# One piece of V per batch loaded into the lower 64 partitions of two slots, in transfers of 8 rows

## The chip, the cores and the metric

The kernel runs on one core of one Trainium2 chip. The metric is device time in microseconds for one execution. Before the change three runs took 1097.45, 1098.14 and 1099.65 us; the median is 1098.14.

## The reference

Eight sequences (B = 8) with one token each (width D = 448) pass through attention, a small MLP block, the same attention and the same MLP again. The attention has 16 query heads on 8 KV heads of 256 dimensions, over a cache of 4096 positions:

```python
q = (x @ wq).reshape(B, 1, 16, 256).transpose(0, 2, 1, 3)
k = jnp.repeat(k_cache, 2, axis=1)              # k_cache: (8, 8, 4096, 256) bf16
v = jnp.repeat(v_cache, 2, axis=1)
p = softmax(einsum("bhqd,bhkd->bhqk", q, k) / 16)
o = einsum("bhqk,bhkd->bhqd", p, v)             # then @ wo, added to x

x = x + attention(layernorm(x)); x = x + mlp(layernorm(x))
x = x + attention(layernorm(x)); x = x + mlp(layernorm(x))
```

Both attentions use the same caches, of 134 MB each. In the MLP of one token the shifted parts of the first half are zero, so that what is left of it is a normalisation, a 448 x 1792 product, a gelu, a 1792 x 448 product and the residual.

## The kernel before, in words

**Pieces and slots.** K or V of one KV head of one batch is 4096 positions x 256. Partition p holds positions 32p to 32p + 31, so that one partition's share is 16 KB in a row of memory. It is cut into four pieces (`c` = 0 to 3) of 128 partitions x 4096 bytes, 512 KB each (`chunks`, L444). Pieces land in 31 slots of SBUF (`NSLOT`, L13), each 128 partitions x 4096 bytes. One, two or four pieces that follow each other can come in one DMA (512 KB, 1 MB, 2 MB) if slots side by side are free. All loads are issued by SyncE (SP), on one queue.

**Order of the work.** Heads are taken in pairs: m = 0 to 3 stands for KV heads 2m and 2m + 1, with s = 0, 1 for the two. For batch b the kernel computes scores, softmax and the product with V in layer 0 (`kpart`, `vpart` with `layer` = 0), then `turn(b)` (output sum, MLP, next query), then layer 1. What was transposed of K for m = 1 to 3 stays in its slots for layer 1; K for m = 0 and all of V are loaded again. Loads of K and V are woven with each other (`weave`, L1213). Layer 1's V for m = 0 of batch b is woven with the first K of batch b + 1 (L1241); for the last batch it comes at the end (L1245).

**A planner decides order and slots.** Every operation is an entry with a cost, a due time and what it depends on (`Plan.add`), every load a `Unit` (L73) with a slot. `Plan.schedule` (L168) runs through the entries in simulated time and writes down the order of each engine's instructions, the slot of each load and the waits. A load is issued when its slots are free, that is when the last reader of what they held has run; it occupies SP for 330 ns in the plan (L292). A group of loads that finds no run of free slots can be split (L266 to L275). So a small change of one cost or one load can move instructions and slots elsewhere.

**K.** Most pieces of K are rearranged by VectorE in blocks of 32 x 32 (L914) and then multiplied on TensorE (L923); some are transposed by TensorE (L832), copied back by ScalarE (L892) and multiplied (L902).

**Softmax.** The scores of a pair lie in PSUM as 128 columns. The exponentials go to `pT` (L1006). In the order that pieces rearranged by VectorE need, they are transposed once more by TensorE and VectorE (L1013, L1021); for pieces that keep their natural order they are computed again into `pT` (L1027), or copied to `pN`, a small tile of which there are two (L399, L1010).

**V.** The product with V in this part of the kernel (L1077 to L1092) takes a 128 x 8 block of exponentials as weights and 512 columns of V as the moving operand, four matmuls per piece, and accumulates in a bank of `psV` over both heads:

```python
w = pN[z][:, 12 * i + 4 * s:12 * i + 4 * s + 8] if own_(s, c) else pT[y][:, o:o + 8]
v = slots[u.slot].rearrange("p (k j d) -> p j k d", k=2, j=4)[:, i]
last = e.matmul(psV[x][32 * i:32 * i + 8, :].rearrange("p (k d) -> p k d", k=2), w, v,
                start=(s == 0 and c == 0), stop=(s == 1 and c == NCH - 1))
```

Another form (L1063) takes V as weights.

**Semaphores.** Each slot has one, which a load raises by 16 when it has landed; a reader waits for the slot's running total (L1264).

Of the kernel before, what the change touches and what calls it, by code (L numbers as in the profile page):

```python
# [3 lines left out]
P = 128  # L4
B = 8
# [6 lines left out]
NCH = 4  # L12
NSLOT = 31  # L13
SMALL = 218
SLOT = 2048
# [5 lines left out]
NN = ((1, 0, 1, 1), (0, 0, 1, 1))  # L21
NZ = 2
WIDE = ((1, 0),)
MOST = (4, 4, 4, 2)
DRY4 = 4000.0
STILL = (False, False)
# [46 lines left out]
class Unit:  # L73


    def __init__(self, name, emit, nbytes, slotted=True):
        self.name, self.emit, self.nbytes, self.slotted = name, emit, nbytes, slotted
        self.wide = None
        self.slot = self.sem = self.val = None
        self.op = None  # L80
        self.readers = []
        self.land = None
        self.evs = [None, None]
        self.raw, self.source = False, None
        self.group, self.lead, self.pair = [self], None, None


class Plan:
# [79 lines left out]
    def schedule(self, order, nslot):  # L168
# [8 lines left out]
        free = {e: 0.0 for e in ("pe", "dve", "act", "pool", "sp")}  # L177
# [68 lines left out]
        while remaining or nxt[0] < len(order):  # L246
# [8 lines left out]
            while nxt[0] < len(order):  # L255
                u = order[nxt[0]]
                if any(d.end is None for d in u.op.deps):
                    break
                start = max(free["sp"], max((d.end + 80 for d in u.op.deps), default=0.0))
                us = u.group  # L260
                if u.slotted:
                    if len(us) == 1:
                        best = single(t)
                    else:
                        best, short = run(t, len(us))
                        if short and len(us) == 4 and transfer < t + DRY4:  # L266
                            order.insert(nxt[0] + 1, self.split(u, users))
                            us = u.group
                            best, short = run(t, len(us))
                        one = single(t)  # L270
                        if (len(us) == 2 and short and transfer < t + DRY and one is not None and slot_free[one][0] <= t + 1e-6
                                and len(slot_free) > bool(raw or u.raw) + sum(1 for o in ready["act"] if o.target is not None)
                                and free["sp"] <= t + 1e-6):
                            order.insert(nxt[0] + 1, self.split(u, users))
                            us, best = u.group, one  # L275
                    held = sum(1 for x in {o.target for o in ready["act"] if o.target is not None} if x.slot is None)
                    if best is None or len(slot_free) < len(us) + bool(raw or u.raw) + held:
                        break
                    start = max([start] + [slot_free[best + k][0] for k in range(len(us))])
                if start > t + 1e-6:  # L280
                    sp_next = start
                    break
                if u.slotted:
                    for k, x in enumerate(us):
                        _, waits = slot_free.pop(best + k)
                        x.slot = best + k
                        for w in waits:
                            u.op.deps[w] = True
                        live.append(x)
                        if x.raw:  # L290
                            raw.add(x)
                free["sp"] = start + 330.0  # L292
                if u.emit is not None:
                    transfer = max(start + 3300.0, transfer) + (P * 4096 * len(us) / 415.0 if len(us) > 1 else u.nbytes / 410.0)
                    land = transfer + 2000.0
                else:
                    land = start
                for x in us:
                    x.land = land
                u.op.on = "sp"  # L300
                seq["sp"].append(u.op)
                done(u.op, land, 0.0)
                nxt[0] += 1
                progress = True
            for e in ("pe", "dve", "act", "pool"):
# [15 lines left out]
                o = min(cand, key=lambda o: (o.prio, o.name))  # L321
# [37 lines left out]
def bass_interleave_layers__gqa_block_cached__mixer_s_mlp__decode_kernel(  # L359
# [26 lines left out]
    slots = [slab[:, SLOT * i:SLOT * i + SLOT] for i in range(NSLOT)]  # L386
# [6 lines left out]
    ident = sb("ident", [P, P], bf)  # L393
# [3 lines left out]
    pT = [sb(f"pT{i}", [P, 192], bf) for i in range(NP)]  # L397

    pN = [sb(f"pN{i}", [P, 48], bf) for i in range(NZ)]  # L399
# [17 lines left out]
    psS = [nc.alloc_psum_tensor(f"psS{i}", [P, 512], f32) for i in range(NS)]  # L417
    psV = [nc.alloc_psum_tensor(f"psV{i}", [P, 512], f32) for i in range(NV)]
# [7 lines left out]
    plan = Plan()  # L426
# [14 lines left out]
    U_wo = [rows(f"wo{i}", wo_sb[:, 8 * i:8 * i + 8, :], wo_src[:, 8 * i:8 * i + 8, :], P * 7168 * 1.1) for i in range(4)]  # L441
    U_w4 = [rows("w4", w4_sb[:, :, :], B_w4.rearrange("(t m) n -> m t n", m=P), P * 12544 * 1.1)]

    def chunks(cache, b, h, name, skip=(), most=2):  # L444


        src = cache[b, h].rearrange("(p j) d -> p (j d)", p=P)

        def emit(e, u):
            c, n = int(u.name[-1]), len(u.group)  # L450
            return e.dma_start(slab[:, SLOT * u.slot:SLOT * (u.slot + n)], src[:, SLOT * c:SLOT * (c + n)])
        us = [None if c in skip else Unit(f"{name}{c}", emit, P * 4096) for c in range(NCH)]
        for i in range(0, NCH, most):
            group = [u for u in us[i:i + most] if u is not None]
            if len(group) == most:
                plan.load(group[0], mates=group[1:])
            else:
                for u in group:
                    plan.load(u)
        return us  # L460


    Bc = Buf()
# [350 lines left out]
    def apart(t):  # L814

        return t.rearrange("p (a c u r) -> p a c r u", a=4, u=3, r=4)[:, :, :, :, 0:3:2]
# [19 lines left out]
    def kpart(at, layer, b, m, kept, most=2):  # L836
# [12 lines left out]
        nS[0] += 1  # L849
        p.x = x  # L850
        p.y = y = free_p.pop(0)
        p.z = z = free_n.pop(0) if layer == 0 and m > 1 else None
        plan.prio = at
        p.K, p.kload = [], []
        for s in range(2):
# [169 lines left out]
        for c in range(nn if z is None else 0):  # L1025
            ss = slice(sum(c >= w for w in nns), 2)
            add("act", lambda e, c=c, ss=ss: e.activation(apart(pT[y])[:, :, c, :, ss], xs.rearrange("p (a c r s) -> p a c r s", a=4, c=4, r=4)[:, :, c, :, ss],  # L1027
                                                          ACT.Exp, scale=INV_SQRT_DH), 230, [], [BpT[y]], [bS[x]], prio=pr, name=n + f"pn{c}")
        add("pool", lambda g: g.partition_all_reduce(db, rs, P, ReduceOp.add), 450, [B_["pm"]], [B_["gm"]], prio=pr + 1, name=n + "db")
        R = add("dve", lambda e: e.reciprocal(rc, db), 70, [B_["gm"]], [Brc[y]], prio=pr + 1, name=n + "rc")  # L1030
        R.deps = {d: data or d.eng == "dve" for d, data in R.deps.items()}
# [2 lines left out]
    def vpart(at, p, still, bank, most, aside):  # L1034
# [2 lines left out]
        own_ = lambda s, c: z is not None and c < p.nns[s]  # L1037
        Bp = lambda s, c: [BpN[z]] if own_(s, c) else [BpT[y], BpZ[y]]
        plan.prio = at
        p.V = [u for s in range(2) for u in chunks(A_v_cache, b, 2 * m + s, f"{n}V{s}", (), most)]  # L1040
        p.vload = [u for u in p.V if u.lead is None]
        if layer == 0:
            out_, bo = o1[b % 2][:, 8 * m:8 * m + 8], Bo1[b % 2][m]
        else:
# [28 lines left out]
        else:  # L1073
# [3 lines left out]
            for s in range(2):  # L1077
                for c in range(NCH):
                    u = p.V[NCH * s + c]

                    def pv(e, u=u, c=c, s=s):
                        for i in range(4):
                            o = 12 * (NCH * i + p.place(s, c)) + 4 * s
                            w = pN[z][:, 12 * i + 4 * s:12 * i + 4 * s + 8] if own_(s, c) else pT[y][:, o:o + 8]
                            if c < p.nns[s]:
                                v = slots[u.slot][:, 512 * i:512 * i + 512].rearrange("p (k d) -> p k d", k=2)
                            else:
                                v = slots[u.slot].rearrange("p (k j d) -> p j k d", k=2, j=4)[:, i]
                            last = e.matmul(psV[x][32 * i:32 * i + 8, :].rearrange("p (k d) -> p k d", k=2), w, v,  # L1089
                                            start=(s == 0 and c == 0), stop=(s == 1 and c == NCH - 1))  # L1090
                        return last
                    o = add("pe", pv, 430, Bp(s, c), [], [bV[x]], [u], prio=at + 0.02 * (NCH * s + c), name=f"{n}V{s}{c}", n=4)  # L1092
                    if s or c:
                        o.deps[first] = True
                    else:
                        first = o
# [24 lines left out]
                for d in Bq1[b].readers + Bq1[b].writers:  # L1121
                    O.deps.setdefault(d, False)
        free_p.append(y)
        if z is not None:
            free_n.append(z)

    Bst = [{k: Buf() for k in ("pm", "gm", "mx")} for _ in range(NS)]
    red, Bred = sf[:, 0:8], [Bs[k] for k in ("sq", "f", "f1")]
# [129 lines left out]
    for o in seq["sp"]:  # L1258
        u = o.unit
        if u.emit is None:  # L1260
            u.sem = None
            continue
        if u.slotted:
            slot_n[u.slot] += 16  # L1264
            u.sem, u.val = slot_sem[u.slot], slot_n[u.slot]
        else:
            u.sem, u.val = nc.alloc_semaphore(f"s_{u.name}"), 16
# [124 lines left out]
```

## Time and profile before

| | |
|---|---|
| profiled execution | 1098.74 us |
| its span, first to last instruction | 1095.7 us |
| TensorE, its weight loads, VectorE, ScalarE, GpSimd busy | 756.3, 526.6, 832.6, 207.8, 71.4 us |
| moved by DMA | 448.94 MB, 410 GB/s on average |
| mean granted TensorE clock | 0.619 |
| loads from V: 2 MB, 1 MB, 512 KB | 50, 149, 14 |
| loads from K: 2 MB, 1 MB, 512 KB | 44, 71, 2 |
| median time from issue to landing, V: 2 MB, 1 MB, 512 KB | 19.1, 9.7, 8.1 us |

How to read it. The page gives each engine's busy time and share of the span, then the span in 40 slices with a digit for the busy tenths. "DMA" is the mean busy share of the core's 16 DMA engines. A queue's line has its packets, its megabytes, and the time of its packets as a share of what 16 engines have in the span. A line of SyncE's own waits has the instruction that waits, who ended the wait, then the total in us, how many times, and the longest. The chain of waits follows the work that ended last back to the start, and shares the span out over what it passed through. Beside these views the trace has a record for each DMA packet (start, duration, size, queue; not which of the 16 engines) and a time for each rise of a load's semaphore; a load of 128 rows makes sixteen rises, one when each DMA engine has finished its share, and has landed with the last.

### The profile page before, as it was taken

The numbers are of one execution on the slowest core, as the hardware profiler recorded it, in microseconds if no ns is written. First come the engines' busy times: TensorE is split into PE (matmuls) and PEld (weight loads), VectorE is DVE, ScalarE is ACT, GpSimd is POOL, SyncE is SP. The second block draws the span as 40 slices with busy tenths as digits, with TensorE's granted clock in tenths as the row PEclk, the third lists the DMA queues.
The fourth block names the chain that finished last, engine by engine and source line by source line (L and its number), as shares of the span: only waits on it lengthen the run. The fifth ranks groups of instructions, "written<-read, shape, count | busy, mean of one in ns | idle before, by whom it ended". The sixth has DMA issues, their size and how long they took to land.

```text
span 1095.7 us, 33703 instructions
## 1 busy us (share of the span) xinstructions
PE 756.3 (69%) x15400; PEld 526.6 (48%) x15400; DVE 832.6 (76%) x1595; ACT 207.8 (19%) x314; POOL 71.4 (7%) x232
## 2 busy tenths in 40 slices
PE   2566586778577865867767787577666786676864
PEld 2355454465346543555436554355444654356533
DVE  4999459964997499955899469984799739995572
ACT  1032121112021211203112032121221121121210
POOL 0000000000000000000000000000100000000000
PEclk9997566556655665556655556555655566555665
DMA  9999999999999999999999999999999999999994
GB/s 353 406 419 420 395 406 426 422 412 408 429 423 415 412 425 427 421 405 409 424 426 420 411 412 429 426 417 394 427 427 423 419 399 428 427 422 411 410 427 176
DMA packets 54846, 448.94 MB, mean 410 GB/s; under 512 B 5536, under 2 KB 11568, under 8 KB 14128
## 3 DMA queue, kind: packets, MB, share of 16 engines
q1 hardware_dynamic: 54704, 446.80, 98.4%
q8 instruction: 120, 1.97, 0.7%
q14 instruction: 22, 0.18, 0.0%
HBM read 446.77 MB, written 0.01 MB: 408 GB/s over the span
## 4 chain that ended last, share of the span: by engine, by line
DVE 39%; DMA 24%; PE 21%; issue 9%; ACT 3%; POOL 0%; POOLq 0%; DVEq 0%
DVE slots L914 29%; DMA slots<-in_A_k_cache_dram 16%; DMA slots<-in_A_v_cache_dram 8%; PE psV L1089 6%; PE psS L923 5%; DVE pT L1021 2%; PE psT L678 2%; ACT slots L892 2%; PE psS L902 2%; DVE slots L1102 1%; PE psV L1063 1%; PE psT L607 1%; PE psK L832 1%; PE psT L1138 1%; DVE qe L643 1%
## 5 line engine op out<-in xcount | busy, mean ns | idle before, releaser
L914 DVE STREAM_TRANSPOSE slots<-slots 128x1024 bf16<-128x1024 bf16 x544 | 649.4, 1228 | 33.0 <-DMA slots<-in_A_k_cache_dram 24.3
L923 PE MATMUL psS<-qe,slots 128*128 128x8 bf16 x5760 | 225.3, 175 | 152.6 <-DVE slots L914 111.5
L923 PEld LDWEIGHTS psS<-qe,slots 128*128 128x128 bf16 x5760 | 191.1, 104 | 238.5 <-DVE slots L914 176.0
L1089 PE MATMUL psV<-slots,pT 128*8 128x512 bf16 x1528 | 181.1, 550 | 17.5 <-DMA slots<-in_A_v_cache_dram 9.5
L892 ACT COPY slots<-psK 128x1024 bf16<-128x1024 bf16 x80 | 78.8, 1014 | 168.0 <-PE psK L832 167.6
L832 PE MATMUL psK<-ident,slots 128*128 128x128 bf16 x640 | 74.2, 301 | 4.2 <-DMA slots<-in_A_k_cache_dram 4.1
L1100 ACT ACTIVATE slots<-psV 128x512 bf16<-128x512 f32 x48 | 29.0, 605 | 218.5 <-PE psV L1089 218.4
L985 POOL PARTITION_ALL_REDUCE small<-small x64 | 23.8, 372 | 693.5 <-DVE small L983 582.4
L832 PEld LDWEIGHTS psK<-ident,slots 128*128 128x128 bf16 x640 | 61.1, 138 | 7.0 <-DMA slots<-in_A_k_cache_dram 4.9
L1063 PE MATMUL psV<-pT,slots 128*128 128x2 bf16 x1568 | 50.9, 166 | 17.1 <-DMA slots<-in_A_v_cache_dram 15.9
L951 PE MATMUL psS<-slots,qe 128*8 128x512 bf16 x184 | 55.4, 587 | 6.7 <-DVE slots L914 5.4
L1063 PEld LDWEIGHTS psV<-pT,slots 128*128 128x128 bf16 x1568 | 47.3, 104 | 19.7 <-DMA slots<-in_A_v_cache_dram 16.1
L1089 PEld LDWEIGHTS psV<-slots,pT 128*8 128x8 bf16 x1528 | 31.5, 90 | 50.5 <-issue 20.9
L1021 DVE STREAM_TRANSPOSE pT<-psS 128x128 bf16<-128x128 bf16 x64 | 44.9, 702 | 6.5 <-PE psS L1013 4.7
L1006 ACT ACTIVATE pT<-psS 128x128 bf16<-128x128 f32 x56 | 15.5, 277 | 178.7 <-DVE psS L1003 178.6
L1066 DVE TENSOR_REDUCE small<-psV 128x8 f32<-128x32 f32 x16 | 2.8, 174 | 58.5 <-PE psV L1063 58.5
L1111 PE MATMUL psV<-same,slots 128*128 128x4 bf16 x320 | 14.0, 166 | 43.0 <-DVE slots L1102 36.9
L630 DVE TENSOR_TENSOR qe<-psT,small 128x32 bf16<-128x32 f32 x32 | 6.1, 190 | 48.2 <-PE psS L923 34.3
L902 PE MATMUL psS<-qo,slots 128*128 128x2 bf16 x768 | 27.8, 167 | 17.6 <-ACT slots L892 10.5
L1102 DVE TENSOR_TENSOR slots<-psV,slots 128x512 bf16<-128x512 f32 x48 | 32.3, 672 | 10.0 <-ACT slots L1100 10.0
L902 PEld LDWEIGHTS psS<-qo,slots 128*128 128x128 bf16 x768 | 24.0, 101 | 25.4 <-ACT slots L892 17.1
L1111 PEld LDWEIGHTS psV<-same,slots 128*128 128x128 bf16 x320 | 11.8, 102 | 49.2 <-issue 40.8
(170 smaller groups left out, 805.8 us busy)
## 6 DMA issues: line engine op xcount, KB each, us to landing
slots<-in_A_v_cache_dram SPq DMA_DIRECT2D x149, 1024.0 KB, 9.7
slots<-in_A_v_cache_dram SPq DMA_DIRECT2D x50, 2048.0 KB, 19.1
slots<-in_A_k_cache_dram SPq DMA_DIRECT2D x44, 2048.0 KB, 18.1
slots<-in_A_k_cache_dram SPq DMA_DIRECT2D x71, 1024.0 KB, 13.7
slots<-in_A_v_cache_dram SPq DMA_DIRECT2D x14, 512.0 KB, 8.1
wo_sb<-in_A_wo_dram SPq DMA_DIRECT2D x4, 896.0 KB, 19.5
wq_sb<-in_A_wq_dram SPq DMA_DIRECT2D x3, 1024.0 KB, 9.1
w_sb<-in_B_w_dram SPq DMA_DIRECT2D x1, 1568.0 KB, 16.9
```

The costliest lines, as they stand in the source:

```text
L832: last = e.transpose(tile[:, j * P:(j + 1) * P], slots[u.slot][:, o:o + P], ident[:, :])
L892: return e.copy(slots[u.slot][:, 1024 * t:1024 * t + 1024], tile)
L902: last = e.matmul(o, slots[u.slot][:, i:i + P], q, start=(cc == 0), stop=(cc == 1))
L914: return e.transpose(o, i)
L923: last = e.matmul(o, slots[u.slot][:, i:i + P], qe[:, 128 * k + 64 * s + 8 * g:128 * k + 64 * s + 8 * g + 8], start=(g == 0), stop=(g == 7))
L951: last = e.matmul(o, q, K[:, lo:hi + 1:hi - lo, :, g, :], start=(g == 0), stop=(g == 7))
L1021: add("dve", lambda e: e.transpose(pZ[:, :, 0:3:2].rearrange("p n s r -> p n r s"), psS[x][:, 128:192].bitcast(bf).rearrange("p (n r s) -> ...
L1063: last = e.matmul(o, slots[u.slot][:, i:i + P], w, start=(j == 0), stop=(j == 7))
L1089: last = e.matmul(psV[x][32 * i:32 * i + 8, :].rearrange("p (k d) -> p k d", k=2), w, v, start=(s == 0 and c == 0), stop=(s == 1 and c == ...
L1100: add("act", lambda e: e.activation(part(0), psV[x][:, :], ACT.Copy), 590, [], [Bhalf[0]], [bV[x]], [v], prio=at - 1, name=n + "ve0").targ ...
L1102: add("dve", lambda e: e.tensor_tensor(part(1), psV[x][:, :], part(0), ALU.subtract), 590, [Bhalf[0]], [Bhalf[1]], [bV[x]], [v], prio=at - ...
L1111: last = e.matmul(to[:, 4 * cc:4 * cc + 4].rearrange("p (s h) -> p s h", s=2), part(k // 2)[:, i:i + P], w, start=(k == 0), stop=(k == 3))
```

## The change

For one piece per batch (piece 3 of V of KV head 0 in layer 1, batches 0 to 6; with bf16 data 512 KB) the 128 rows no longer go to the 128 partitions of one slot. Rows 0 to 63 go to partitions 0 to 63 of one slot and rows 64 to 127 to partitions 0 to 63 of a second slot; partitions 64 to 127 of both stay unused. Each half comes in eight DMAs of 8 rows, to partitions r0, r0 + 4, ..., r0 + 28, with r0 = 0 to 3 and 32 to 35, so that 16 small DMAs take the place of the piece's share of a larger one. The other pieces of that head come at most two in one DMA.

Since V's rows 64 to 127 now lie in partitions 0 to 63, their exponentials must too: one more matmul with a part of the identity moves them down into PSUM, ScalarE copies them to a tile `pN`, and the product of this piece is eight matmuls of 64 rows instead of four of 128. The planner counts eight issues of 330 ns for each half.

```diff
+LOWS, LOWC = 0, 3
+def LOW(layer, b, m, s):
+    return s == LOWS and m == 0 and layer == 1 and b < B - 1
...
-                free["sp"] = start + 330.0
+                free["sp"] = start + 330.0 * u.issues
...
+        if low:
+            def half(p0):
+                def emit(e, u):
+                    for i in range(8):
+                        r0 = 32 * (i // 4) + i % 4
+                        d = e.dma_start(slots[u.slot][r0:r0 + 29:4, :], src[p0 + r0:p0 + r0 + 29:4, SLOT * LOWC:SLOT * (LOWC + 1)])
+                        if i < 7:
+                            d.then_inc(u.sem, 16)
+                    return d
+                return emit
+            most = 2
+            us[LOWC] = Unit(f"{name}{LOWC}", half(0), 64 * 4096)
+            us[LOWC].upper = Unit(f"{name}u{LOWC}", half(64), 64 * 4096)
+            us[LOWC].issues = us[LOWC].upper.issues = 8
...
+        p.zl = zl = free_n.pop(0) if p.low else None
...
+            low = psS[x][0:64, 192:208].rearrange("p (a r) -> p a r", a=4)
+            add("pe", lambda e: e.matmul(low, ident[:, 64:P], apart(pT[y])[:, :, p.place(LOWS, LOWC), :, LOWS], start=True, stop=True),
+                110, [BpT[y], Bc], [], [bS[x]], prio=pr, name=n + "lo", n=1)
+            add("act", lambda e: e.copy(apart(pN[zl])[0:64, :, 0, :, LOWS], low), 230, [], [BpN[zl]], [bS[x]], prio=pr, name=n + "lc")
...
+                    def low(e, u=u, c=c, s=s):
+                        for i in range(4):
+                            o, i_ = 12 * (NCH * i + p.place(s, c)) + 4 * s, 12 * i + 4 * s
+                            for w, v in ((pT[y][0:64, o:o + 8], u), (pN[p.zl][0:64, i_:i_ + 8], u.upper)):
+                                last = e.matmul(psV[x][32 * i:32 * i + 8, :].rearrange("p (k d) -> p k d", k=2), w,
+                                                slots[v.slot][0:64].rearrange("p (k j d) -> p j k d", k=2, j=4)[:, i], start=False, stop=False)
+                        return last
...
-            slot_n[u.slot] += 16
+            slot_n[u.slot] += 16 * u.issues
```

## The prediction

> **What bounds the kernel now.** I read the page's DMA parts first, since the engines' rows leave room and these do not.
>
> ```profile
> PE 756.3 (69%) x15400; PEld 526.6 (48%) x15400; DVE 832.6 (76%) x1595; ACT 207.8 (19%) x314; POOL 71.4 (7%) x232
> ...
> DMA  9999999999999999999999999999999999999994
> ...
> q1 hardware_dynamic: 54704, 446.80, 98.4%
> q8 instruction: 120, 1.97, 0.7%
> ```
>
> The sixteen DMA engines are busy in every slice but the last; VectorE, the busiest engine, idles 24%. The second queue, q8, carries 120 blocks of 16 KB of instructions, and what follows hangs on which DMA engines carry them.
>
> The trace's packet records (start, duration, bytes, no engine's number) and its landings (sixteen completions for a load of 128 rows, one from each DMA engine) say more:
> - From completion to completion a 1 MB load takes 2.485 us (median of 160), a 2 MB load 4.894 (84), a 512 KB load 1.25. There are 223, 94 and 16 of them, and the remaining weight loads take 21 us by their own steps: 554 + 460 + 20 + 21 = 1055 us for each DMA engine.
> - The completions of the load that lands at 21.5 us lie within 0.69 us. The first block starts at 22.2 us, and in the next load one completion is 1.81 us behind the first. At 107 us, after eight blocks and one of 8 KB (q14), nine are 1.4 to 2.2 us behind and seven within 0.6. All lags together have grown by 12.95 us: 1.52 us for each 16 KB.
> - The blocks' own durations repeat with period eight (1107, 1086, 1026, 1028, 1075, 1071, 1061, 1105 ns, then 1099, 1082, 1021, 1032, 1081, 1075, 1060, 1099). So eight DMA engines take them in turn, 15 each: 15 x 1.52 = 22.9 us that the other eight do not spend.
> - 1055 + 22.9 = 1078 us, and from the first packet of a large load (2.2 us) to the last landing (1082.2 us) it is 1080. The loaded eight wait some 2 us in the whole run, so they set the time. The other eight wait where loads are issued just in time: at 748 us their completions lie within 1.2 us, those of the loaded eight 2.3 to 4.3 us behind; at 766 us most of the gap is gone.
>
> Who issues just in time is seen in SyncE's own waits:
>
> ```profile
> SPq L451 <- PE psV L1089: 284.6, 83, 11.8
> SPq L451 <- PE psS L923: 255.8, 79, 11.2
> ```
>
> A load waits for a slot that TensorE frees. And the chain of waits shows how far the compute is from being the limit itself:
>
> ```profile
> DVE 39%; DMA 24%; PE 21%; issue 9%; ACT 3%; POOL 0%; POOLq 0%; DVEq 0%
> ```
>
> Only 24% is DMA: compute and loads close a loop, and a faster DMA pays in full only where that loop has slack.
>
> **The change part by part.** The profiled execution took 1098.74 us: a span of 1095.7 and 3.0 around it; the median of the runs is 1098.14, so I subtract from 1098.1.
>
> *Fewer bytes on one half.* Seven times a 512 KB piece comes as sixteen loads of 8 rows instead of a quarter of a 2 MB load (in the first batch, half of a 1 MB load). An 8-row load runs on eight DMA engines: the load of x (8 rows) shows eight late completions, 0.82 to 0.90 us after a first increment that needs no data. Call these eight the low eight. The upper eight carry nothing of the piece. The 2 MB load becomes 1 MB, 512 KB and the piece: 4.894 - 2.485 - 1.25 = 1.16 us less on the upper eight in six batches, 1.25 in the first; three other 2 MB loads split in two (3 x 0.08 more), as the two instruction orders side by side show. Sum: 6 x 1.16 + 1.25 - 0.23 = **8.0 us off the upper eight**.
>
> *More on the low eight.* They get sixteen rows instead of eight: 2 x 1.25 - 1.16 = 1.34 us per batch, 9.4 in all, and the fixed part of 112 small loads. A 1 MB load's step exceeds eight packets of 0.306 by 0.037 us; for a packet of its own the nearest rows are x's 896-byte packets (39 to 61 ns, 41 inside large loads), so I take 0.037: 4.1 us. Upper bound: the two 256 KB loads of wq's tail, whose steps are 1.08 and 1.17 us against 0.62 for their bytes, 0.5 us over; lower bound 0. Sum: **+13.5 us on the low eight** (9.4 to 65).
>
> *Which eight are loaded with blocks?* The trace names no DMA engine. If the upper eight are, they come to 1078 - 8.0 = 1070.0 and the low eight to 1055 + 13.5 = 1068.5: nearly even, the time falls by 8.0. If the low eight are, they come to 1078 + 13.5. **This is the assumption on which the forecast stands**; no row decides it. I put it at five to one: a block stays on eight fixed engines in turn, which looks like a half set aside, and a half that is set aside for the system's own traffic is more likely the one that short transfers, which fill engines from one end (x's eight), leave alone. That is a judgement, not a reading. [...]
>
> *SyncE.* 112 issues take the place of 7 parts of issues. One takes 0.33 us (median), back to back 0.43 and 0.04 between; eight take 3.4 to 3.8. The loads at these places land 13.5 us (issue at 172.5 us) and 15.5 us (280.8) after their issue, while the DMA still runs on where this is 6.3; 7 us of cover against 3.8, so nothing. If the cover were gone: 14 x 3.8 = 53 us.
>
> *Slots.* The piece holds two slots, each half empty, of 31: up to 1.25 us less queued ahead, against the same 7 us. Nothing; uncovered, 7 x 1.25 = 9 us.
>
> *Compute.* Per batch four more matmuls on psV (L1089 589 ns, the same 512 columns on half the rows; 2.4 us), one like the transpose at L1013 (286 ns) and one small ScalarE copy (L1027: 183 to 330 ns) before V's product: 3.0 us per batch, 21 in all uncovered. TensorE is busy 5.1 and 5.7 of 10 us at 180 and 200 us; behind the copy only that one product is queued, and V's products come in order after it. Nothing gained below zero: no operation is dropped. I cost it at 0, with up to 1 us per batch if the later release of the two slots holds a load in the just-in-time stretch.
>
> *Given back.* Eight times per run the queue is nearly empty. There the loaded engines have almost no slack beyond the gap that now vanishes. If the loop through TensorE does not come earlier, part of a batch's 1.16 us is lost as idling; between 0 and all 8, I take 1, since the queue stands at 13 us and more through most of a batch, and landings that come earlier free slots earlier.
>
> Sum: 1098.1 - 8.0 + 1 = **1091**.
>
> **Rivals.**
> 1. *The compute sets the pace at the seven turns* and the gain is idled away: 1098. For: DVE 39% of the chain, and VectorE busy 10.0 of 10 us from 180 to 210. Against: the loaded eight's budget closes to 2 us in 1080.
> 2. *The blocks run on the low eight, or on some of them.* Place: the low eight's queue in all seven batches; price: + 13.5 us on engines with 2 us of slack: 1111. It decides from one loaded engine among the low eight on, as a load has landed when its last engine has. For: nothing in the trace names engines. Against: only the judgement above.
> 3. *Small loads cost the low eight more than 0.037 us each.* They start 22.9 us ahead; 9.4 + 112 c passes that at c = 0.12 us, and there the time is the old one; at c = 0.2 it is 1098 + 9 = 1107. For: wq's tail, 0.5 over. Against: the 512 KB loads follow at 1.25 us, and w3's tail of 112 KB at 0.34 to 0.62, so fixed parts of queued loads overlap. [...]
> 4. *The 8-row loads spread over sixteen engines*, and nothing shifts: 1098 and a little. Against: x's eight completions. Counted with rival 1.
>
> **How the numbers follow.** Forecast 0.62 (1088.5 to 1095); rivals 1 and 4 together 0.10 (within 2 us of 1098, which is the 0.2% that a measurement of this kernel can tell from no change); rival 3 0.12, of which two thirds lie below 1105; rival 2 0.16 (1107 to 1115). The range from 1088.5 to 1105 holds forecast, rivals 1 and 4 and most of rival 3, and leaves out rival 2 and the rest of rival 3: 0.80 of the cases. The forecast's own range is 1088.5 to 1095. Faster 0.62, same 0.10, slower 0.28.
>
> **What would show it.** Right: the last large load lands some 7 us sooner after the first packet than the 1080 us here; the sixteen completions before a just-in-time stretch within some 2 us instead of 4.3; GB/s over the span up by 0.6%. Rival 2: completions spread by 6 us and more after a piece, in the same order. Rival 3: long gaps between 4096-byte packets. Rival 1: the same span with completions close together, and the sixteen engines' share below 98.4%. What makes it wrong first is the naming of the eight.

## The result and the profile after

The changed kernel takes 1107.89 us (median of five runs, 1107.31 to 1109.33), the kernel before 1097.62 in the runs beside it (1097.09 to 1099.65). The ratio is 1.0094 (95% interval 1.0079 to 1.0109): 10.3 us slower, where 7 us faster was forecast. The profiled execution is the one of 1107.89 us, with a span of 1106.1.

The page of the changed kernel, the lines that the prediction showed of before:

```profile
PE 763.1 (69%) x15427; PEld 526.8 (48%) x15427; DVE 832.8 (75%) x1595; ACT 208.5 (19%) x321; POOL 71.5 (6%) x232
...
DMA  9999999999999999999999999999999999999994
...
q1 hardware_dynamic: 57792, 446.80, 98.2%
q8 instruction: 121, 1.98, 0.7%
```

The engines do what they did before (TensorE 6.8 us more, VectorE 0.2). The same 446.80 MB come in a span 10.4 us longer. The last large load lands at 1092.6 us; before it landed at 1082.2. So the loads are late, and by the whole of it.

SyncE's waits and the chain:

```profile
SPq L459 <- PE psV L1129: 252.7, 66, 8.4
SPq L459 <- PE psS L949: 229.3, 76, 11.2
```

```profile
DMA 35%; DVE 33%; PE 20%; issue 7%; ACT 2%; SPq 0%; POOL 0%; POOLq 0%; DVEq 0%
```

SyncE waits less for slots (252.7 and 229.3 us against 284.6 and 255.8). In the chain DMA grows from 24% to 35% and VectorE falls from 39% to 33%: compute now waits for loads more often.

Where? The windows view sums each engine over a stretch; its last three columns are the granted TensorE clock, the share of the sixteen DMA engines' time and what they moved. Two rows of before, then the same of after, from piece to the just-in-time stretch that follows it:

```profile
300.00:340.00 40.00, 28.74 (x555) 20.05 (x555) 39.01 (x55) 8.58 (x12) 3.04 (x10) 0.54 1.01 422
340.00:380.00 40.00, 31.42 (x725) 22.89 (x725) 17.44 (x68) 9.76 (x13) 2.00 (x6) 0.66 1.00 408
```

```profile
300.00:340.00 40.00, 28.56 (x542) 19.35 (x542) 38.43 (x55) 8.65 (x13) 3.04 (x10) 0.55 1.01 423
340.00:380.00 40.00, 29.99 (x706) 22.20 (x704) 18.15 (x68) 6.49 (x10) 2.00 (x6) 0.59 0.98 376
```

While the queue is deep (300 to 340 us) both move the same. In the just-in-time stretch the changed kernel moves 376 GB/s where before moved 408: 32 GB/s x 40 us = 1.3 MB, 3 us of transfer. The other just-in-time stretches cost less: where the same number of bytes has moved, the profiled changed kernel is 0.3 us behind at 280 us, 0.7 at 340, 3.6 at 380, 5.3 at 530, 7.0 at 780 and 10.6 at 1080, so a price per piece below is a mean over unequal batches. A busy share of 0.98 stands there beside 376 GB/s, and some packets are recorded longer (those of 8192 bytes from 355 to 375 us 0.36 us on average, 0.31 from 300 to 340), so the share is no measure of idling here; GB/s is.

The sixteen completions of a load show what precedes this. The lags behind the first, in ns, for a load ahead of the second piece (it lands at 295.0 us) and for one behind it (308.7 us), in the changed kernel:

```
ahead   0 124 168 219 297 308 390 691 833 891 1383 1622 1774 2734 2862 2951
behind  0 223 520 726 1435 1598 2204 2370 2494 2589 2667 2673 2676 3761 5112 5334
```

Eight lags moved on by 2.37 us (0, 124, 219, 297, 308, 1383, 2734 and 2951 became 2370, 2494, 2589, 2667, 2676, 3761, 5112 and 5334) and seven back by 0.17, since one of these is now the first. So the eight fell 2.54 us behind the seven: sixteen packets of 4096 bytes, which follow each other at 0.161 us. One (833 to 2204) fell 1.54 behind them: a block. The eight that got the piece include two of the three that were last already. The spread goes from 3.0 to 5.3 us (the prediction's sign of rival 2 was 6 and more), and as a load has landed when its last engine has, every later load lands with those two until the just-in-time stretch.

Theory after this: each low engine gets sixteen packets of 0.161 us in place of 1.16 us, 1.42 us more per batch, 9.9 in seven, and engines at the end of the queue are among them. Rivals: computation or slots, SyncE's issues, the small loads themselves.

### The profile page after: what moved, and what is told of

It is laid out like the page before. It is cut to its first block, busy times and chain, and to the rows that moved or that the text cites. A ratio compares the mean times of both kernels' runs of the same rounds, so it can differ in the third digit from the quotient of the medians.

```text
span 1106.1 us, 33891 instructions
## 1 busy us (share of the span) xinstructions
PE 763.1 (69%) x15427; PEld 526.8 (48%) x15427; DVE 832.8 (75%) x1595; ACT 208.5 (19%) x321; POOL 71.5 (6%) x232
## 3 DMA queue, kind: packets, MB, share of 16 engines
q1 hardware_dynamic: 57792, 446.80, 98.2%
## 4 chain that ended last, share of the span: by engine, by line
DMA 35%; DVE 33%; PE 20%; issue 7%; ACT 2%; SPq 0%; POOL 0%; POOLq 0%; DVEq 0%
DVE slots L940 23%; DMA slots<-in_A_k_cache_dram 23%; DMA slots<-in_A_v_cache_dram 12%; PE psV L1129 6%; PE psS L949 4%; DVE pT L1047 2%; PE psT L702 2%; ACT slots L918 1%; PE psT L631 1%; PE psV L1095 1%; PE psS L928 1%; DVE slots L1145 1%; PE psK L856 1%; PE psT L1182 1%; DVE qe L667 1%
## 5 line engine op out<-in xcount | busy, mean ns | idle before, releaser
L977 PE MATMUL psS<-slots,qe 128*8 128x512 bf16 x192 | 53.1, 588 | 5.5 <-DVE slots L940 5.5
L1182 PE MATMUL psT<-small,wo_sb 128*128 128x1 bf16 x1024 | 33.2, 166 | 2.6 <-DVE small L1158 1.5
```

What stands on the lines that cost most here:

```text
L977: last = e.matmul(o, q, K[:, lo:hi + 1:hi - lo, :, g, :], start=(g == 0), stop=(g == 7))
L1182: last = e.matmul(psT[:, 4 * (2 * s + i) + c:4 * (2 * s + i) + c + 1], wo_sb[:, a, d0:d0 + P], o1[b % 2][:, a:a + 1], start=(k == 0), stop ...
```

## The experiments

### 1 and 2. Which engines carry the blocks

Loads of four bytes per row, with 8, 4, 2 and 1 rows (probes), were put behind four loads of the kernel before; a load of k rows makes k late rises (x's load of 8 rows eight, 0.82 to 0.90 us after its first; the 8-row and 4-row probes below eight and four), so its rises say how far k of the engines stand behind.

```diff
+                    for (j, k), s_ in PROBES.items():
+                        if j == count[0]:
...
+                            eng.dma_start(probe[0:k, c:c + 2], A_x[0:k, 0, 0:2]).then_inc(s_, 16)
+                    count[0] += 1
```

> The kernel before with sixteen probes: at four places late in a batch, where the completions of a load spread most, loads of 8, 4, 2 and 1 rows of 4 bytes follow that load. A probe runs on as many DMA engines as it has rows and has a semaphore of its own, so its landings show how far behind just these engines are. Theory A (the blocks of instructions run on some of the low eight and on some of the others): of the eight landings of the 8-row probe some, about four, lie in the lagging group of the sixteen completions ahead of it, over 1.5 us behind its first. The forecast's assumption (the upper eight carry the blocks): all eight within 1.3 us. All blocks on the low eight: all eight in the lagging group. The probes of 4, 2 and 1 rows then say which. Time: within 1 us of before.

1097.65 us. At 998 us the sixteen lags were 0 to 3606 ns; the 8-row probe found its engines at 0, 170, 235, 1740, 2034, 2486, 3090 and 3388, the 4-row probe at 0, 235, 2034 and 2486. (A rise is given here as the lag of the load that it stands behind, since each probe moves it on by some 0.19 us.) In every place both early and late engines were among the eight, which speaks against a half without blocks. The second run had 14, 12, 10, 8, 7, 6, 5 and 4 rows in the same places; what a probe has and its smaller neighbour has not is one engine or two:

```diff
-    PROBES = {(j, k): nc.alloc_semaphore(f"s_pr{j}_{k}") for j in (122, 200, 240, 318) for k in (8, 4, 2, 1)}
+    PROBES = {(j, k): nc.alloc_semaphore(f"s_pr{j}_{k}") for j in (122, 200, 240, 318) for k in (14, 12, 10, 8, 7, 6, 5, 4)}
```

> The kernel before with eight probes of 14, 12, 10, 8, 7, 6, 5 and 4 rows, four bytes each, behind the loads 122, 200, 240 and 318. A probe of k rows makes k late rises, and each shows how far one of the k engines that it uses stands behind. Two probes of neighbouring k differ by the engines in between, so the set of lags tells engine by engine which ones lag. From the first probes: engines 0 to 3 lead, two of engines 4 to 7 lag and two do not, six of engines 8 to 15 lag. Theory (the blocks go round eight neighbouring engines): the two that lag are 6 and 7, and the two of the upper eight that do not lag are 14 and 15. Rival: the loaded engines are scattered, in which case no neighbouring set of eight fits. The time is that of the kernel before, 1098 us, within 2 us; 32 issues of SyncE take 0.3 to 0.6 us each and are covered by some 13 us of queue.

1098.90 us. At 340 us, after eight blocks of 16 KB since 272 us that each moved one lag on by some 1.5 us, eight lags are small (0 to 788) and eight large (1964 to 3630):

```
sixteen lags              0 170 207 476 526 626 671 788 1964 1991 2412 2422 2672 3338 3402 3630
engines 0-4, 7            small
engines 5, 6              1964, 1991
engines 8, 9              one small (476), one large (2412 or 2422)
engines 10, 11            the other of 2412 and 2422, and 2672
engines 12, 13            3630 and one of 3338 and 3402
engines 14, 15            one small (671), and the other of 3338 and 3402
```

At 602 us (eight lags of 0 to 1918, eight of 2468 to 3858) the same engines are small and large. I read from this that 5, 6, 10 to 13, one of 8 and 9 and one of 14 and 15 carry the blocks of 16 KB: six of the upper eight, two of the low eight. The theory of eight neighbours (6 to 13) falls: 7 carries none, 5 does. The numbers are only names for these sets, as no record names an engine: 0 to 3 are the four that the 4-row probe finds (in the first run its four lags are among the eight of the 8-row probe), 4 is the one that the 5-row probe adds, and so on up; 8 and 9 are the two that the 10-row probe adds to the low eight.

In the other two places the lags do not part so cleanly: one of engines 0 to 3 stands at 2311 of 3783 ns at 735 us, and at 2951 of 4503 at 998 us. The trace shows a reason. Besides the 120 blocks of 16 KB the kernel before has 22 of 8 KB, on another queue:

```profile
q14 instruction: 22, 0.18, 0.0%
```

The lag of 2951 was 1987 before the 8 KB block at 992 us and 2936 after it. In the first run the 2486 that the 4-row probe found was 1551 before the 8 KB block at 992 us and 2469 after it. So in these places an 8 KB block ran on an engine that carries none of 16 KB, and set it back by some 0.9 us. "Without blocks" below means without those of 16 KB.

### 3. The changed kernel's last engines

Probes in the changed kernel, two loads behind the piece's second half:

```diff
+                        if count.get(j) == 2:
...
+                            eng.dma_start(probe[r:r + k, c:c + 2], B_w1[0:k, 0:2]).then_inc(s_, 16)
```

> The changed kernel with probes of 12, 10, 8, 7, 6, 5 and 4 rows, four bytes each, two loads behind the second half of the piece in batches 1, 2, 4 and 5. From the probes in the kernel before, engines 5 and 6, one of 8 and 9, 10 to 13 and one of 14 and 15 carry the blocks. Theory (the low eight's two loaded engines set the pace of the changed kernel): engines 5 and 6 stand last, 1.5 us or more behind every other engine, in most of these places; and the loaded engines of the upper eight are no longer last. Rival (all engines wait for each other in these loads): engines 5 and 6 are not among the last. Time: that of the changed kernel, 1108 us, within 2.

1110.63 us, one run, 2.7 above the changed kernel where 2 was the most expected, with 28 probes in it. In all four places the two last engines of sixteen are the ones that a 7-row probe shows and a 5-row probe does not, 5 and 6:

```
after the piece of batch   lag of engines 5 and 6 (ns)   next engine
1                          5149, 5342                    3481
2                          5107, 5692                    3115
4                          4154, 5203                    3950
5                          4000, 4982                    3271
```

The changed kernel goes at the pace of these two. Each time at least one is 1.2 us and more behind the other fourteen; the 1.5 us that I expected of both held in two places.

### 4. The same load without the change

The product and the piece's load as before; rows 0 to 63 of the piece are loaded once more into a second slot, by eight loads of 8 rows, and by eight loads of 4 rows.

```diff
+            def again(e, u):
+                for i in range(8):
+                    r0 = 32 * (i // 4) + i % 4
+                    d = e.dma_start(slots[u.slot][r0:r0 + 29:4, :], src[r0:r0 + 29:4, SLOT * LOWC:SLOT * (LOWC + 1)])
...
-        p.low = LOW(layer, b, m, LOWS)
+        p.low = False
```

> The computation of the kernel before, and the piece in one load of 128 rows as before; beside it, rows 0 to 63 of the same piece are loaded a second time by eight loads of 8 rows into a second slot, which nothing reads (V's product only waits for it). It adds to the low eight engines eight packets of 4096 bytes per batch, 8 x 0.161 = 1.29 us by the packets of the changed kernel, and nothing to the upper eight; no matmul and no copy is added, and SyncE issues nine loads for the piece instead of seventeen parts. Theory (at least one engine of the low eight carries blocks and sets the pace, the rest of the change costs nothing): +7 x 1.29 = 9.0 us and 0.6 for the split loads, 1107 to 1108. Rival A (the change's time comes from the computation or from the two half-empty slots): 1098 to 1100. Rival B (it comes from SyncE's sixteen issues per batch): half of the change's 10.3 us, 1103.

> As the run with loads of 8 rows, with 4 rows in each of the eight loads, so that only engines 0 to 3 get the eight further packets, again 8 x 0.161 = 1.29 us per batch. The slots, the waits and the eight issues of SyncE are the same. Theory (engines 0 to 3 carry no blocks and stand 2 us and more ahead of the last): 1098 to 1099, no change but for the split loads (up to 0.6 us). Rival A (the time of the changed kernel comes from issues or slots): the same time as the run with 8 rows. Rival B (all of the low eight set the pace): 1107, too.

With 8 rows 1108.98 us against 1098.57, ratio 1.0093 (1.0079 to 1.0107): 10.4 us. With 4 rows (`r0:r0 + 13:4`) 1099.38, ratio 1.0006 (0.9997 to 1.0015): 0.8 us, not told from none. Same slots, same number of issues, same waits; the difference is that engines 4 to 7 get the packets too, and with them twice the bytes. That is worth 9.6 us, and 7 x 1.29 = 9.0 are packets. So a load on these engines alone, with none of the rest, makes a slowdown as large as the change's. The rivals "slots" and "SyncE's issues" fall as the main cause: one more slot and eight issues per batch stand at 0.8 us, and the change's sixteen were not tested apart. Of the stretch from 340 to 380 us, first with 8 rows, then with 4:

```profile
340.00:380.00 40.00, 31.69 (x741) 23.41 (x740) 18.96 (x69) 7.42 (x10) 2.00 (x6) 0.59 0.99 395
```

```profile
340.00:380.00 40.00, 32.80 (x765) 23.86 (x762) 18.46 (x70) 9.04 (x12) 2.00 (x6) 0.59 1.01 410
```

With 4 rows it moves what the kernel before moved (408).

### 5. The computation alone

```diff
-                            for w, v in ((pT[y][0:64, o:o + 8], u), (pN[p.zl][0:64, i_:i_ + 8], u.upper)):
+                            for w in (pT[y][0:64, o:o + 8], pN[p.zl][0:64, i_:i_ + 8]):
...
-            us[LOWC] = Unit(f"{name}{LOWC}", half(0), 64 * 4096)
...
```

> The computation of the changed kernel alone: the move of the exponentials by a matmul and a copy, and eight matmuls of 64 rows instead of four of 128, with the piece in one load of 128 rows and one slot. It multiplies rows 0 to 63 of those pieces with both sets of weights and leaves rows 64 to 127 out of the product. Theory (the computation is covered by the DMA engines' work): 1098 to 1099. Rival (the computation sets the pace at the turns): up to 3.0 us per batch, 21 us, at most 1119; if it made the whole of the change's time, 1108.

1099.36 us, ratio 1.0006 (0.9997 to 1.0015). The move of the exponentials, eight matmuls and the split loads together cost 0.8 us (-0.3 to 1.6). That rival falls.

### 6. The change in three batches

```diff
-    return s == LOWS and m == 0 and layer == 1 and b < B - 1
+    return s == LOWS and m == 0 and layer == 1 and b in (0, 2, 4)
```

> The changed kernel with the piece in batches 0, 2 and 4 only: three instead of seven. Theory A: each piece adds 1.42 us to DMA engines that have no slack, 3 x 1.42 = 4.3, so 1101 to 1103. A cost that comes once, by another order of the work: anything, not in proportion.

1102.86 us against 1098.44, ratio 1.0042 (1.0028 to 1.0056): 4.4 us for three pieces, 1.47 each; seven cost 10.3, also 1.47. By the intervals it is 1.0 to 2.1 with three and 1.2 to 1.7 with seven, so the exact agreement is luck. But the cost grows with the number of pieces, and its mean is near the 1.42 of the packets.

### 7. Other ways to cut the piece

Each half in one load of 64 rows (then in the same two slots), and the whole piece in one slot by eight loads of 16 rows:

```diff
-                    for i in range(8):
-                        r0 = 32 * (i // 4) + i % 4
...
+                    return e.dma_start(slots[u.slot][0:64, :], src[p0:p0 + 64, SLOT * LOWC:SLOT * (LOWC + 1)])
```

> The changed kernel, but each half of the piece comes in one load of 64 rows, which sixteen DMA engines share at 4 rows each: the two half-empty slots, the eight smaller matmuls, the copy and the split of the 2 MB loads stay, the uneven load of the DMA engines and the small transfers go. Theory A (uneven load): 1098 to 1100. Theory C (slots, compute and splits cost the time): 1106 to 1109. If writing only the lower 64 partitions holds the DMA engines up as the 64-row tail of wq did, 0.5 us for each half: 1105.

```diff
+                for i in range(8):
+                    d = e.dma_start(slots[u.slot][i:i + 121:8, :], src[i:i + 121:8, SLOT * 3:SLOT * 4])
```

> The kernel before, but the same piece comes in eight loads of 16 rows over all 128 partitions of one slot, issued one after the other like those of the change; slots, matmuls and the share of each DMA engine are as before. Theory A: 1097.5 to 1099.5. Theory B (a small load has a cost of its own on the DMA engines, 0.1 us or more): 8 x 0.1 x 7 = 5.6 us or more, 1103 and up. Theory C' (the issues hold SyncE up): between, with SyncE's issues seen to come late where the queue is short.

1132.28 us, ratio 1.0297 (1.0267 to 1.0327), and 1117.70, ratio 1.0177 (1.0150 to 1.0204): both far slower than theory A had it; the first lies outside every theory, the second only within theory B, which was open above. Their 4096-byte packets, counted from 150 us on, 159 ns in the changed kernel (25th to 75th percentile 159 to 160), reach 301 and 285 ns at the 90th percentile, and 850 and 502 of the neighbouring loads' 16 KB packets take over 1.2 times their 611 ns, against 49 in the changed kernel. My guess was that engines hold each other up where they write the same half of the partitions; no record says which engine writes which partitions. One more run changes the partitions alone: the 8-row loads of experiment 4 go to partitions 64 to 127 instead of 0 to 63.

```diff
-                    d = e.dma_start(slots[u.slot][r0:r0 + 29:4, :], src[r0:r0 + 29:4, SLOT * LOWC:SLOT * (LOWC + 1)])
+                    d = e.dma_start(slots[u.slot][64 + r0:64 + r0 + 29:4, :], src[r0:r0 + 29:4, SLOT * LOWC:SLOT * (LOWC + 1)])
```

> The run that loads rows 0 to 63 a second time by eight loads of 8 rows, with one thing changed: they go to partitions 64 to 127 of the second slot instead of 0 to 63. [...] Theory (engines that write the same partitions' side hold each other up, which made the loads of 64 rows and of 16 rows slow): 4096-byte packets above 1.2 x 159 ns by the hundred (115 where they went to partitions 0 to 63), upper neighbours slowed too, and a time above that run's 1109: up to 8 x 0.16 = 1.3 us more per batch, 1111 to 1118. Rival (what made those two slow was the splitting into loads of 16 or 64 rows, whatever the partitions): the same 1109.

1127.70 us, ratio 1.0256 (1.0234 to 1.0278), 28.3 us above the kernel before, where the loads to partitions 0 to 63 cost 10.4: 17.9 us, 2.6 per batch, for other partitions and nothing else. 464 packets of 4096 bytes and 597 of 16 KB take over 1.2 times their normal time from 150 us on, against 115 and 65 there. The DMA view from 280 to 320 us, each figure the GB/s of one us, first with partitions 0 to 63, then with 64 to 127:

```profile
GB/s 418 393 451 401 434 475 459 393 426 393 401 393 418 414 418 467 455 410 442 397 406 479 422 410 442 442 377 459 410 442 410 442 442 426 410 426 442 393 459 377
```

```profile
GB/s 442 426 410 393 426 442 459 401 467 426 410 385 418 422 397 393 459 459 459 426 377 414 238 283 246 295 254 172 410 426 393 459 410 426 442 410 459 442 410 410
```

For six us the rate falls to 172 to 295, against 377 to 479 in the first row. That the partitions alone set this price is shown, and the rival (the same 1109) falls. That engines hold each other up there remains a guess: the neighbouring loads' packets are slowed as well (597 of 16 KB against 65), but no record names the engine of a packet. The price was twice what I gave. The loads of 64 and of 16 rows fit the guess, but what their split costs by itself was not taken apart. The change itself, whose low eight write partitions 0 to 63, has no such loss (21 slow packets of 4096 bytes from 150 us on).

### 8. A piece on engines without 16 KB blocks

If a block-free engine is 22.9 us ahead over the run, the piece belongs on engines 0 to 3. In five batches it went to partitions 0 to 15 and 32 to 47 of four slots, in eight loads of 16 rows whose source is written as 4 x 4 rows, which I took to put four rows on each of engines 0 to 3; then, in seven batches, half of its columns only.

```diff
+                    for h in range(2):
+                        d = e.dma_start(slots[u.slot][32 * h:32 * h + 16, :],
+                                        src[32 * q + 16 * h:32 * q + 16 * h + 16, SLOT * LOWC:SLOT * (LOWC + 1)].rearrange("(i j) d -> j i d", i=4))
```

> [...] The product is that of the kernel before and reads the first of the four slots only, so it leaves out three quarters of the piece's rows. Engines 0 to 3, which carry no blocks, get 32 x 0.161 - 1.16 = 4.0 us more per batch, 20 in all, against some 22.9 that the blocks cost the others; the other twelve, all loaded ones among them, get 1.16 us less, 5.8 in all. Theory (the loaded engines set the time, wherever they sit): 1098.5 - 5.8 = 1093, up to 1096 if engines 0 to 3 fall behind by 2 us for a while after each piece or the four slots cost some of the queue. Rival A (a load confined to few engines costs time whatever these carry, by issues, slots or splits): 1099 to 1104. [...]

```diff
+            def left(e, u):
+                return e.dma_start(slots[u.slot][:, 0:W], src[:, SLOT * LOWC:SLOT * LOWC + W])
...
+                        d = e.dma_start(slots[u.slot][32 * (q % 2):32 * (q % 2) + 16, W * (q // 2):W * (q // 2) + W],
+                                        src[p0 + 16 * q:p0 + 16 * q + 16, SLOT * LOWC + W:SLOT * (LOWC + 1)].rearrange("(i j) d -> j i d", i=4))
```

> Half the dose of the run with quarters, in all seven batches: of the piece's 4096 bytes per row the first 2048 come in one load of 128 rows, the other 2048 of all rows in eight loads on engines 0 to 3, into partitions 0 to 15 and 32 to 47 of two further slots (the product is that of the kernel before and reads the second half of the piece from the first slot, where it was not loaded). The other twelve engines get 8 x 0.08 = 0.64 us less per batch, less 0.08 for the split load: 0.5, 3.5 to 4 in all; engines 0 to 3 get 32 x 0.08 - 0.6 = 1.9 to 2.0 more. In the run with quarters engines 0 to 3 stood 4.7 us behind the rest from one piece to the next just-in-time stretch, where the others waited for them; ahead of the piece the spread was 2.8. Theory (what one engine is ahead is worth only as far as it stands ahead at that moment, 1 to 3 us, since a lead is lost in each just-in-time stretch): between 1095 and 1099, faster only if the lead exceeds 2.5 us in most batches. Rival A (the lead adds up over the run, 22.9 us, and the run with quarters was slow for its slots or loads): slots and loads as there, 1107 to 1110. Rival B (the sum over the run alone decides): 1094.5.

1110.50 us, ratio 1.0106 (1.0089 to 1.0123): 12 us slower, where 5 faster was expected. And 1104.27, ratio 1.0055 (1.0041 to 1.0068): 5.7 us slower, outside what the theory gave. Each of the small loads made one rise at once and four late, so they did run on four engines; that these are engines 0 to 3 is assumed, as no record names them. It is not the loss of experiment 7 either (31 slow packets of 4096 bytes, against 834 with eight loads of 16 rows).

The lags, in us, tell why. With half the columns, the last load ahead of the second piece, then one behind it:

```
ahead   0 0.2 0.3 0.3 0.3 0.6 1.0 1.4 1.4 1.4 1.8 1.9 2.1 2.2 2.2 2.5
behind  0 0.2 1.0 1.4 1.4 1.4 1.8 1.9 2.0 2.1 2.2 2.5 2.9 3.0 3.0 4.9
```

Four lags moved on by 2.7 us (32 packets of 84 ns): three from 0.3, and one from 2.2. An engine without blocks stood 0.3 us from the last one: that is where the theory of the second run, which took engines 0 to 3 to be 1 to 3 us ahead, was out. The trace offers a reason: an 8 KB block at 272 us moved a lag of 1.2 us to 2.2, where this one stood. With quarters the load that lands at 327 us has twelve lags up to 2.6 and four of 5.5 to 7.3; these four stay last to the just-in-time stretch, where the others wait for them, and at 388 us the whole spread is 2.6 again. So a lead does not add up to 22.9 us: it lasts from one just-in-time stretch to the next, and how much of it there is differs by engine.

How much room engines 0 to 3 have per batch follows from three doses, as (packets added) - (relief of the others) - (time lost per batch). Eight packets of 159 to 162 ns: 1.29 - 0 - 0.8/7 = 1.2. Half columns: 2.69 - 0.5 - 5.7/7 = 1.4. Quarters: 5.1 - 1.16 - 12/5 = 1.5. Three doses, one room of 1.2 to 1.5 us (the first is a floor, as its 0.8 us is not told from none), against 0 for the low eight with engines 5 and 6, where 22.9 over eight batches would be 2.9. It is an estimate, and what two to four more slots cost is in it, which was not taken apart. It leaves little to win here, and none of these kernels beats the one before.

In the quarters kernel's window the loss stands in the same place as in the changed one:

```profile
300.00:340.00 40.00, 28.79 (x522) 19.50 (x519) 38.40 (x55) 8.48 (x12) 3.05 (x10) 0.54 1.01 421
340.00:380.00 40.00, 29.32 (x691) 21.96 (x689) 21.26 (x70) 5.52 (x8) 2.01 (x6) 0.60 0.98 376
```

## Why the prediction was wrong

**What bounds the kernel.** Right: a price of 1.42 us per piece on two DMA engines reached the time nearly whole.

**Which eight are loaded with blocks.** This is the step that failed: "If the upper eight are, they come to 1078 - 8.0". They are, but for two: engines 5 and 6 of the low eight carry blocks too, they stand last in the changed kernel (experiment 3), and small loads that reach them cost 10.4 us where those on engines 0 to 3 cost 0.8 (experiment 4). Rival 2 had it ("or on some of them", "it decides from one loaded engine among the low eight on"), and its mechanism took place; its price of 13.5 us was too high by the next point. The odds of five to one rested on a picture of two halves, and no row supported that; nor did a row show then that short transfers fill the engines from one end (in experiment 2 the 4-row probe's four lags are among the 8-row probe's eight). Small loads of k rows behind a large one (experiment 2) would have told it ahead of the forecast.

**The lead of the other eight.** By experiment 8 this would have failed too. "They start 22.9 us ahead" took a sum over the run for something to draw on at any moment. The prediction had named the reason itself (the other eight wait where loads come just in time) and did not carry it through. It also counted no 8 KB block against the other eight; the 8 KB blocks, seen on them in experiment 2, take some 0.9 us each from the lead of one. With the room of 1.2 to 1.5 us per batch that engines 0 to 3 showed, a piece that adds 2.58 and relieves the others by 1.16 would come out near 0 even with every block on the upper eight: an estimate, since no arrangement here has that.

**More on the low eight.** 9.4 + 112 c with c = 0.037 gave 13.5. The packets follow each other at 0.161 us for 0.159 of data: c is nearer 0.005 (16 x 0.161 - 1.16 = 1.42, 9.9 in seven), so rival 3 falls for these loads. The upper bound of 65 us, taken from wq's tail, is not absurd: small loads cost 28.3 us in the last run of experiment 7, but 17.9 of that came with the partitions, not with the small loads.

**SyncE.** The issues were mis-sized, and it cost nothing:

```profile
L459 SPq DMA_DIRECT2D slots<-in_A_v_cache_dram x221: 327/328/11222, 6.8 to 1064.4; - x111
L466 SPq DMA_DIRECT2D slots<-in_A_v_cache_dram x112: 623/623/707, 168.7 to 935.1; - x112
```

The first line has the loads of 128 rows, the second those of 8; lowest, median and longest are in ns. An 8-row load takes 0.62 us, 0.67 from one to the next, against the 0.33 and 0.43 that I took from loads of 128 rows; sixteen take 10.7 us, not 6.8 to 7.6. The queue covered it (the load behind the second piece still landed 14 us after its issue), and with eight issues per batch on four engines only 0.8 us remained.

**Slots, computation.** Forecast at 0; the runs leave 0.8 us for computation and split loads, and 0.8 for one slot, eight issues and split loads, both with 0 in the interval.

**Given back.** Taken as 1 us of a gain; there was no gain to give back. But the stretch that it named is where the loss appears.

## What to carry to other kernels

Here a large load landed with the last of its sixteen rises, and an uneven load cost about what it added to the engines that were last at that moment (1.47 us per piece, for 1.42 added); a sum over the run per engine does not show that, and a lead lasted only until the queue next ran dry (in experiment 8 four lags of 5.5 to 7.3 us at 327 us, the whole spread 2.6 at 388). Find out which engines are last, by small loads of k rows behind a large one, before moving bytes between them. And test which partitions such loads write: the same eight small loads per batch cost 10.4 us in partitions 0 to 63 and 28.3 in 64 to 127; why was not shown.

## What the runs showed of the hardware

- Eight of sixteen DMA engines carry the 16 KB instruction blocks, but not one half of them: two among the eight that 8-row loads use, none among the four that 4-row loads use (read from the probes and the lags at 340 us, eight of 0 to 788 ns and eight of 1964 to 3630). In two traced places an 8 KB block ran on one of these four, and set it back by 0.9 us (a lag of 1987 ns became 2936, one of 1551 became 2469).
- Queued 4096-byte packets of 8-row loads follow at 0.161 us, for 0.159 of data, so 112 small loads had no visible fixed cost on the engines; on SyncE each took 0.62 us, about twice a load of 128 rows (0.33).
- 512 KB in two loads of 64 rows cost 4.8 us more per piece than its share of a load of 128 rows (33.8 us in seven), and the loads around it are slowed with it (850 packets of 16 KB over 1.2 times their 611 ns, 49 in the changed kernel).
- A load of 16 rows whose source is written as 4 x 4 rows runs on four engines: one rise at once and four late.
